# Second-level products and accumulating DMAs in the first pair of a cross-network kernel

## Chip, cores, metric

The kernel runs on one core of one Trainium2 chip. The metric is the device time of one execution in microseconds (us). The time before is 2277.18 us (median of 3 runs, 2277.13 to 2278.06).

## The reference, cut to what matters

```python
# x0: 16384 x 1024 bf16, ws: 6 x 1024 x 1024 bf16, bs: 6 x 1024 bf16
x = x0
for l in range(6):
    proj = jnp.einsum('bd,de->be', x, ws[l]) + bs[l]
    x = x0 * proj + x
```

## The kernel before

The 16384 rows are done in 16 pairs of two blocks of 512 rows; a pair goes through six layers, so there are 96 layer passes. Each pass multiplies by a 1024 x 1024 matrix in Winograd's form of Strassen's scheme: seven products with half-size blocks, called 1 to 7, instead of eight. Four of the seven need a sum of weight blocks. Such a sum is the same for all 16 pairs, so the first pair (pair 0) makes it on VectorE and saves it to DRAM (`Lc`); the other 15 pairs only load it. Pairs 1 to 15 also cut products 5 and 2 a second time into seven quarter-size products ("two levels"). Their weight sums are called 5i and 2i and are made in pair 0 as well.

```python
RING = 16                                         # weight tiles of 0.52 MB
level1 = lambda u: units[u][0] == 0 or u == NU - 1    # pair 0 and the last pass: one level
RAW = [("4", "load"), ("w12", "stage"), ("1", "load"), ("2", "load")]
MAKE = [(w, "make") for w in ("5", "6", "7", "3")]
...
            combo("5", "w12", "4", ADD, ())       # on VectorE, then saved
            combo("6", "5", "1", SUB, ("5",))
            combo("7", "1", "w12", SUB, ())
            combo("3", "2", "6", SUB, ("6",))
            for X, s in (("2i", isum[2 * (l % 2)]), ("5i", isum[2 * (l % 2) + 1])):
                icombo("5", lambda a=a, sv=sv: tt(sv[:, 0], a(0, 1), a(1, 1), ADD), ())
                icombo("6", lambda a=a, sv=sv: tt(sv[:, 1], sv[:, 0], a(0, 0), SUB), "5")
                icombo("3", lambda a=a, sv=sv: tt(sv[:, 2], a(1, 0), sv[:, 1], SUB), "6")
                icombo("7", lambda a=a, sv=sv: tt(sv[:, 3], a(0, 0), a(0, 1), SUB), ())
                save(X, lambda s=s: s, [rn(i) for i in "5637"])
```

Every operation carries a rank, which is its planned time in microseconds from the start of its layer. The program is emitted in the order of these ranks, and each engine (SyncE, which issues most DMAs, GpSimd, which issues the rest, ScalarE, VectorE, TensorE) works off its own list strictly in that order. An operation that is not ready holds all later ones of its engine, whatever they need.

## Time and profile before

| | kernel before |
|---|---|
| time, median of 3 runs | 2277.18 us |
| span of the profiled run | 2275.2 us |
| TensorE / VectorE / ScalarE busy | 100% / 91% / 81% |
| DMA issues in pair 0 from GpSimd | 36 plain saves, 6.2 and 6.9 us to landing (median) |

This is the table by stretch of the kernel before. Behind the stretch stand its length and, for PE (TensorE), PEld (its weight loads), DVE (VectorE), ACT (ScalarE) and POOL (GpSimd), the busy microseconds with the number of instructions; then come the granted TensorE clock, the busy share of the DMA engines, and what they moved in GB/s.

```profile
20.00:60.00 40.00, 39.63 (x184) 18.00 (x184) 39.06 (x46) 28.08 (x48) 8.17 (x12) 1.00 0.86 305
60.00:100.00 40.00, 40.00 (x187) 18.09 (x185) 39.10 (x45) 27.31 (x48) 4.76 (x9) 1.00 0.83 227
100.00:140.00 40.00, 40.00 (x187) 18.16 (x186) 38.92 (x43) 27.14 (x47) 3.71 (x7) 1.00 0.60 207
```

TensorE never stops and runs at full clock, VectorE is nearly full, and the DMA engines are busy 60 to 86% of the time. (Shares a little over 1 occur, as overlapping packets are both counted.) From 17 to 150 us the share is 0.75 on average, so some 33 us of DMA time are idle there. That is the room into which the change puts its new transfers.

### The profile page before, as it was taken

The page shows a single profiled execution, that of the slowest core. Times are in us where ns is not written, and L with a number is a line of the kernel's source. Part 1 is how long each engine was busy: PE and PEld are TensorE (multiplying, and loading weights), DVE is VectorE, ACT ScalarE, POOL GpSimd, SP SyncE. Part 2 cuts the span into 40 slices and gives each one's busy share as a digit, 9 for nine tenths or more (in the row PEclk, how much of TensorE's full clock was granted, in tenths as well). Part 3 has the DMA queues.
Part 4 walks back from the last instruction along what each step waited for, and adds up shares of the span by engine and source line. Part 5 has one row for each costly group of instructions (what it writes and reads, how often), then busy time and mean ns, then how long its engine had stood idle before and what let it go on. Part 6 is the DMA issues. An engine that isn't in the chain of part 4 may idle for free.

```text
span 2275.2 us, 34978 instructions
## 1 busy us (share of the span) xinstructions
PE 2265.4 (100%) x12951; PEld 1264.0 (56%) x12951; DVE 2079.9 (91%) x2326; ACT 1839.4 (81%) x3228; POOL 22.1 (1%) x43
## 2 busy tenths in 40 slices
PE   9999999999999999999999999999999999999998
PEld 4455555555555555555555555555555555555554
DVE  7999999999999999999999999999999999999997
ACT  5678888888888888888888888888888888888887
POOL 1110000000000000000000000000000000000000
PEclk9999999999999999999999999999999999999999
DMA  9779797796977969779697796978969689696872
GB/s 279 229 270 289 261 242 269 219 301 209 252 257 221 288 217 260 250 226 283 213 274 241 228 283 204 273 245 230 283 200 292 226 232 286 194 303 216 241 240 65
DMA packets 625868, 557.01 MB, mean 245 GB/s; under 512 B 397600, under 2 KB 552224, under 8 KB 625696
## 3 DMA queue, kind: packets, MB, share of 16 engines
q1 hardware_dynamic: 618864, 534.58, 79.1%
q0 software_dynamic: 5184, 18.88, 2.2%
q8 instruction: 101, 1.65, 0.3%
q10 hardware_dynamic: 1648, 1.32, 0.2%
q14 instruction: 71, 0.58, 0.1%
HBM read 436.22 MB, written 52.43 MB: 215 GB/s over the span
## 4 chain that ended last, share of the span: by engine, by line
PE 98%; DVE 1%; SPq 0%; DMA 0%; issue 0%; ACT 0%; DVEq 0%
PE pA L285 57%; PE pX L389 24%; PE pX L285 16%; DVE ev L198 1%; SPq L529 0%; DMA wp<-in_ws_dram 0%; DVE xst L198 0%; DVE T L198 0%; DVE ti L198 0%; DVE wp L198 0%; SPq L538 0%; ACT ev L294 0%; DVE x0T L487 0%; DVEq L608 0%; DVEq L198 0%
## 5 line engine op out<-in xcount | busy, mean ns | idle before, releaser
L285 PEld LDWEIGHTS <-wp 128*128 128x128 bf16 x7904 | 772.3, 98 | 843.7 <-issue 3.9
L285 PE MATMUL pA<-T,wp 128*128 128x512 bf16 x4608 | 1054.9, 379 | 0.5 <-DVE T L198 0.5
L294 ACT ACTIVATE ev<-pA,b_all 128x512 bf16<-128x512 f32 x1124 | 704.8, 690 | 211.8 <-PE pA L285 211.4
L389 PEld LDWEIGHTS <-wp 128*128 128x128 bf16 x4984 | 487.1, 98 | 156.6 <-issue 15.2
L198 DVE TENSOR_TENSOR ev<-ev,x0T 128x2048 bf16<-128x2048 bf16 (+2 forms) x484 | 482.7, 999 | 8.1 <-ACT ev L294 1.5
L198 DVE TENSOR_TENSOR xst<-ev,xst 128x2048 bf16<-128x2048 bf16 x319 | 388.9, 1219 | 18.6 <-DVE ev L198 0.5
L389 PE MATMUL pX<-ti,wp 128*128 128x256 bf16 x2848 | 397.6, 272 | 0.0
L198 DVE TENSOR_TENSOR ev<-ev,ev 128x2048 bf16<-128x2048 bf16 (+1 forms) x283 | 343.7, 1215 | 26.7 <-ACT ev L294 9.8
L294 ACT ACTIVATE ev<-pX,b_all 128x512 bf16<-128x512 f32 x412 | 289.4, 705 | 59.9 <-PE pX L285 49.3
L285 PE MATMUL pX<-xst,wp 128*128 128x512 bf16 x1376 | 336.4, 379 | 0.0
L285 PE MATMUL pA<-xst,wp 128*128 128x512 bf16 x1280 | 313.5, 379 | 0.0
L290 ACT COPY pX<-pA 128x512 f32<-128x512 f32 x412 | 256.3, 625 | 44.7 <-PE pA L285 44.3
L290 ACT CAST ev<-pX 128x512 bf16<-128x512 f32 x384 | 224.8, 619 | 49.0 <-ACT ev L294 37.6
L198 DVE TENSOR_TENSOR ev<-iu,ip 128x1024 bf16<-128x1024 bf16 x178 | 122.4, 688 | 120.7 <-ACT iu L290 120.7
L290 ACT COPY pX<-pX 128x512 f32<-128x512 f32 x356 | 208.7, 587 | 8.4
L290 ACT CAST iu<-pX 128x512 bf16<-128x512 f32 x356 | 196.8, 639 | 0.0
L198 DVE TENSOR_TENSOR T<-xst 128x2048 bf16<-128x2048 bf16 x160 | 194.8, 1217 | 0.3
L198 DVE TENSOR_TENSOR T<-xst,T 128x2048 bf16<-128x2048 bf16 x160 | 194.5, 1216 | 0.0
L389 PE MATMUL pX<-T,wp 128*128 128x256 bf16 x1068 | 160.2, 273 | 0.0
L290 ACT CAST ip<-pX 128x512 bf16<-128x512 f32 x178 | 104.7, 589 | 54.1 <-PE pX L389 54.1
L389 PE MATMUL pX<-xst,wp 128*128 128x256 bf16 x888 | 133.2, 273 | 0.0
L198 DVE TENSOR_TENSOR xst<-ev,x0T 128x2048 bf16<-128x2048 bf16 x64 | 78.2, 1222 | 1.6
(44 smaller groups left out, 624.3 us busy)
## 6 DMA issues: line engine op xcount, KB each, us to landing
wp<-Lc SPq DMA_DIRECT2D x538, 512.0 KB, 4.6
wp<-in_ws_dram SPq DMA_DIRECT2D x285, 512.0 KB, 5.3
out_dram<-x0T SPq DMA_DIRECT2D x30, 1024.0 KB, 8.6
Lc<-wp POOLq DMA_DIRECT2D x24, 512.0 KB, 6.2
Lc<-isum POOLq DMA_DIRECT2D x12, 512.0 KB, 6.9
w<-in_ws_dram SPq DMA_DIRECT2D x5, 512.0 KB, 6.3
wp<-in_ws_dram ACTq DMA_DIRECT2D x2, 512.0 KB, 5.8
out_dram<-x0T SPq DMA_DIRECT2D x2, 512.0 KB, 3.6
```

What stands on the lines that cost most here:

```text
L198: nc.vector.tensor_tensor(out=o, in0=a, in1=b, op=op)
L285: nc.tensor.matmul(bank[:], lhsT=wt[(u, w)][:, k, m * P:(m + 1) * P], rhs=rhs[:, k, :], start=(start and k == 0), stop=(k == KH - 1), skip ...
L290: add(name, lambda: nc.scalar.copy(out=dst, in_=src), rd, wr)
L294: add(name, lambda: nc.scalar.activation(out=dst, in_=src, func=IDENT, bias=b_all[:, c:c + 1], scale=1.0), rd, wr)
L389: nc.tensor.matmul(pX[bank][:, m * NQ:(m + 1) * NQ], lhsT=wv[:, k, m * P:(m + 1) * P], rhs=rhs[:, k, :], start=(start and m == 0 and k == ...
```

## The change

In layers 2 to 5 of pair 0 the change goes to two levels, as the later pairs do. VectorE has no time for that, so the weight sums of these layers move to the DMAs. A base block is loaded (SyncE), where needed ScalarE changes its sign, and then GpSimd issues an accumulating DMA that adds a second block to it: 5 = w12 + w4, 7 = -w12 + w1, 6 = -w4 + (7), 3 = w2 + (6). Of the small sums for the second level, two of four are done in the same way on quarter blocks. Layers 0 and 1 stay at one level, and all ranks of pair 0 are new. The saves move from GpSimd to SyncE. Weight 4 gets two buffers of its own, and weights w12 (layers 0 and 1), 7 and 6 (layer 2) lie in `xst` memory that pair 1 uses later. The diff, cut to its core:

```diff
+    NONE = 2
-    level1 = lambda u: units[u][0] == 0 or u == NU - 1
+    level1 = lambda u: u < NONE or u == NU - 1
+    ADDED = [(w, "load") for w in ("5", "2", "7", "6", "3", "1")] + [("4", "four")]
+    BASE = {"5": "w12", "7": "w12", "6": "4", "3": "2"}
...
-                    nc.gpsimd.dma_start(Lc[l, CIDX[w]]...            # saves
+                def fn(eng=nc.gpsimd if first and len(w) == 1 else nc.sync):
...
+                for w in "76":
+                    for h in range(2):
+                        add(f"n{w}.{h}", ... nc.scalar.activation(... func=IDENT, scale=-1.0), ...)
+                def accum(w, src, more=(), weights=()):
+                    add("d" + w, ... nc.gpsimd.dma_start(out=raw(w)[:], in_=src(), accum_op=ADD), ...)
+                accum("5", lambda l=l: w_src(l, "4"))
+                accum("7", lambda l=l: w_src(l, "1"))
+                accum("6", lambda raw=raw: raw("7")[:], [f"w{u}.7"], "7")
+                accum("3", lambda raw=raw: raw("6")[:], [f"w{u}.6"], "6")
...
+                        add(X + i + "l", ... nc.sync.dma_start(dst(), part(w)), [], [rn(i)])
+                        if X == "5i":
+                            add(X + i + "a", ... nc.gpsimd.dma_start(out=dst(), in_=part("4"), accum_op=ADD), ...)
+                        add(X + i + "m", ... nc.gpsimd.dma_start(out=dst(), in_=more(), accum_op=ADD), ...)
... (the new ranks of all layers of pair 0 are left out)
```

## The prediction

> **What bounds the kernel now.** I read the page first (busy shares), then the chain of work that ended last, then tables of busy time by stretch, then the groups of instructions, and last the timeline of TensorE at the start. The page says PE busy 100%, DVE 91%, ACT 81%, and that the chain that ended last is 98% PE. A busy PE is only a bound if its matmuls follow each other at their own pace, so I take the pace from the chain (columns: start, duration, what):
>
> ```profile
> 68.87 10.36 PE pA L285 x48
> 93.05 10.36 PE pA L285 x48
> 117.22 10.36 PE pA L285 x48
> ...
> 1766.37 8.63 PE pA L285 x40
> 1789.81 8.63 PE pA L285 x40
> ```
>
> 48 matmuls of 512 columns take 10.36 us, so 0.2158 us each. The same place of two neighbouring layers of the first pair lies 117.22 - 93.05 = 24.17 us apart: this is 112 x 0.2158 = 24.17, seven products of 16 matmuls with no gap. In a later pair, where products 5 and 2 are cut once more, the distance is 1789.81 - 1766.37 = 23.44 us (80 full matmuls and 56 of 256 columns). So a layer costs 24.17 us with one level and 23.44 us with two, and each is pure TensorE time.
>
> Stalls exist only at the very start (TensorE's timeline; the bracket is idle time before it and what ended it):
>
> ```profile
> 12.81 2.85 PE L285 MATMUL pX<-x0T,wp 128*128 128x512 bf16 x12 [1.26 <-ACT pX L290]
> ...
> 17.98 1.90 PE L285 MATMUL pX<-T,wp 128*128 128x512 bf16 x8 [0.49 <-DVE wp L198]
> 20.36 10.52 PE L285 MATMUL pA<-T,wp 128*128 128x512 bf16 x48 [0.49 <-DVE T L198]
> 30.72 3.62 PE L285 MATMUL pX<-x0T,wp 128*128 128x512 bf16 x16
> 34.17 3.62 PE L285 MATMUL pA<-xst,wp 128*128 128x512 bf16 x16
> ```
>
> Layer 0 runs from 6.78 to 34.17 us, 27.4 us for 24.2 us of matmuls. After that nothing holds TensorE until the tail. Whether it can go to two levels earlier is a question for VectorE and the DMAs (table by stretch: length, busy time and count of each engine, clock, DMA share, GB/s; a layer of the first pair, then one of the second):
>
> ```profile
> core 0: us, PE busy (x) PEld busy (x) DVE busy (x) ACT busy (x) POOL busy (x), PEclk, DMA share, GB/s
> 117.20:140.60 23.40, 23.40 (x111) 10.56 (x109) 22.90 (x26) 16.56 (x28) 1.07 (x2) 1.00 0.53 169
> 188.40:211.90 23.50, 23.50 (x134) 12.95 (x133) 21.29 (x24) 20.13 (x36) 0.00 (x0) 1.00 1.14 253
> ```
>
> VectorE is busy 22.90 of 23.40 us in the first pair: it makes the weight combinations beside the layer's own sums. That is why the first pair has one level only.
>
> **What the Trainium skill says.** "TensorE: Matmul & The Clock Gate", section "Wait — 56ns, not 53.3ns?", gives 215.7 ns start to start for 512 columns at full clock; the trace agrees (0.2158 us, granted clock 1.00). "VectorE: DVE Perf Modes", section "The perf-mode tier table (the rule you actually need)", gives 1224 ns for a 2048-element bf16 two-tensor operation; the trace has 1217 ns for a weight combination. "DMA: Bandwidth & Descriptors", section "SWDGE vs HWDGE vs iDMA", says an accumulate during a DMA can only be issued from GpSimd, and its subsection "Issuing engines are not separate DMA queues" that all issuers share the same 16 DMA engines. No accumulating DMA is in this trace, so its price is not measured; that is the weakest spot here.
>
> **The change part by part.** Layers 0 and 1 stay at one level and are re-ordered; layers 2 to 5 of pair 0 get two levels.
>
> 1. TensorE, removed: 4 layers x (24.17 - 23.44) = 4 x 0.73 = 2.9 us. All of it is on the path, as there are no gaps there.
>
> 2. VectorE. The groups with shapes kept apart:
>
> ```profile
> L198 DVE TENSOR_TENSOR wp<-wp 128x2048 bf16<-128x2048 bf16 x12 | 14.6, 1217 | 0.0
> L198 DVE TENSOR_TENSOR isum<-wp 128x512 bf16<-128x512 bf16 x24 | 9.8, 417 | 1.8 <-DMA wp<-in_ws_dram 1.8
> ```
>
> A layer has four large combinations and eight small ones. In a row they start some 1.14 and 0.34 us apart in the timeline, so 4 x 1.14 + 8 x 0.34 = 7.3 us per layer. The change leaves four small ones (1.4 us) and takes 5.9 us away. Two levels add the six operations that prepare the second level's inputs (2 x (0.60 + 0.34 + 0.34) = 2.6 us), two closing sums (2 x 0.60) and one full sum (1.14), together 4.9 us. VectorE thus ends about 1 us lower in a layer that is 0.7 us shorter: still some 95% busy. Without the move to DMA it would need about 28 us in 23.4 us. So the move is what makes the second level possible; by itself it saves no time.
>
> 3. ScalarE: 6 more evictions (34 for 28) and 4 sign changes of 128 x 1024. The second pair's layer shows 20.13 us busy of 23.50 us; four sign changes of about 1 us (estimate from 690 ns for 512 columns) come to 24 us when counted in full, but these records overlap: evictions start 0.5 to 0.6 us apart, so about 34 x 0.55 + 4 = 23 us at most. Tight, but the negations lie up to two layers ahead, and those of layers 2 and 3 partly in one-level layers (16.56 us busy).
>
> 4. DMA, added per layer 2 to 5: loads go from 4 to 7 of 0.52 MB plus four quarter parts (+2.1 MB); four accumulates of 0.52 MB and six of 0.13 MB (2.9 MB). That is 5 MB a layer, 20 MB in all. In the stretch from 17 to 150 us the old kernel moved 240 GB/s x 133 us = 32 MB at share 0.75. 52 MB in some 131 us is 395 GB/s. In the stretch 150 to 179 us, with its DMAs busy all the time, the old kernel reached 388 GB/s, with pieces of 400 to 430. So the DMA engines go from 75% to full in the first pair, even if an accumulated byte costs no more than a copied one. If it costs double (it reads both operands), 12 MB more, about 28 us of DMA time, are in demand.
>
> 5. Small waits that I expect by following the new order: the change frees no time in layer 0, whose first 13.6 us hang on the arrival of x0 and of the two weight quarters as before, so its 3.2 us of stall stay. In layer 1, VectorE does 23 operations from the last half combination (17.9 us) to the layer's T1, 23 us of work plus dependent pairs that start 1.25 instead of 1.14 us apart; T1 is ready 0.3 to 0.4 us after TensorE has finished products 1 and 2 at 41.1 us. Layer 2 begins with inner products that want the difference of T1 early: another 0.4 us. Layers 3 to 5: together 0.3 us. Sum about 1.1 us.
>
> 6. Not touched: 89 later layers (23.44 us each), the last layer and the tail. Moving weight 4 to its own two buffers gives the ring one free place, but TensorE never waits for a weight there, so it is worth 0.
>
> Sum: -2.9 + 1.1 = -1.8 us, from 2277.2 to 2275.4 us.
>
> **The rivals.** (a) The DMA engines become the bound in the first pair. For it: step 4, and two transposing loads of x0 that fall into layer 3 and block the SyncE queue for 20 us in the old timeline. Against it: accumulates are issued 10 us or more ahead of their use (layers 3 to 5: 12 to 20 us by the order's ranks), saves of combinations are due only in the second pair, and the ring of 16 weights gives two layers, some 46 us, of lead. A backlog of 10 us would vanish there; one of 30 to 40 us (the doubled price) would stall TensorE late in pair 0 and early in pair 1 by perhaps 2 to 10 us: 2278 to 2286 us. (b) Head-of-line blocking: GpSimd's and SyncE's queues now hold waits for each other (load, negate, accumulate, accumulate from the result, save). One late link delays all behind it; VectorE too, as 5i7 of layer 2 reads an accumulated weight. I expect 0 to 3 us. (c) All is hidden and the small waits of step 5 do not come: 2277.2 - 2.9 = 2274.3 us. (d) VectorE stays the hidden bound and the two-level layers run at its pace: it would have to lose more than 1 us per layer to waits; up to +2 us.
>
> **Range and chances.** I give the clean outcome (2274.3 to 2276) about 60%, small stalls (2276 to 2280) 25%, a real DMA shortage 15%. The weighted middle is a little over the sum: 2275.9 us, eight in ten between 2274.0 and 2281.5 us. Two per cent are 45.5 us; the whole gain in sight is 2.9 us, so faster by over 2% is nearly excluded (0.003), and slower by over 2% would need the first pair's 145 us to grow by a third (0.012). Within 2%: 0.985.
>
> **What would show it right or wrong.** Right: layers 2 to 5 lie 23.4 to 23.9 us apart on TensorE; VectorE's operations that write wp drop from 25 (two of them halves) to 9; DMA share near 1 from 30 to 150 us; TensorE's waits over 17 us sum to about 1.1 us more than now and name DVE T or ti. Step 4 is wrong if accumulates of 0.52 MB land within 7 us and the share stays under 0.9; rival (a) is right if TensorE waits for the DMA of wp or isum, above all in layers 4 to 6; rival (b), if VectorE or ScalarE waits for a DMA while the DMA share is below 1. The prediction fails if accumulates run far slower than copies, or if the second pair starts with its ring empty.

## The result

The changed kernel takes 2351.04 us (median of 4 runs, 2339.95 to 2353.0), beside 2277.62 us of the kernel before in the same rounds. The ratio is 1.031, with a 95% interval of 1.028 to 1.034. (A ratio here is the mean time of one kernel's fast runs over the mean of the other's of the same rounds, so it is not quite the ratio of the medians quoted.) The result is correct. The change costs 73 us; the prediction was 2275.9 us with 2274.0 to 2281.5 as its range, so it was wrong. The profiled run is the fastest of the four: its span is 2338.1 us, 62.9 more than before.

**Where the time went.** The chain of work after pair 0 has the old pace: the same long run of TensorE starts at 304.74 and at 1782.46 us, 63 layers apart, which is 23.46 us per layer (before: 242.07 and 1766.37 us, 65 layers, 23.45 us). From 242.07 to 304.74 is 62.7 us, so all of the loss lies before 305 us. The table by stretch of the changed kernel:

```profile
20.00:60.00 40.00, 38.20 (x177) 17.09 (x176) 37.48 (x46) 31.91 (x53) 21.66 (x15) 1.00 1.13 323
60.00:100.00 40.00, 22.84 (x120) 12.15 (x119) 18.03 (x24) 15.61 (x27) 11.62 (x11) 0.80 1.05 282
100.00:140.00 40.00, 15.39 (x69) 8.12 (x69) 15.64 (x18) 16.08 (x25) 8.87 (x8) 0.64 1.23 234
140.00:180.00 40.00, 35.31 (x193) 19.01 (x192) 30.35 (x38) 31.08 (x54) 9.92 (x9) 0.96 1.13 288
```

Now the DMA engines are the ones that never stop (share over 1 in every row), while TensorE works 38 of 80 us in the two middle rows. Note the last number: full DMA engines move only 234 to 323 GB/s here. The kernel before moved 388 GB/s with full engines (150 to 179 us).

TensorE's stalls are few and long. These lines are from its timeline (start, duration, what, and in brackets the idle time before it and what ended it):

```profile
69.30 1.01 PE L455 MATMUL pX<-ti,isum 128*128 128x256 bf16 x4 [8.05 <-DVE ti L216]
...
107.52 5.55 PE L313 MATMUL pA<-T,w 128*128 128x512 bf16 x16 [15.51 <-ACT ev L322]
...
134.22 1.01 PE L455 MATMUL pX<-T,wp 128*128 128x256 bf16 x4 [15.50 <-ACT pX L318]
172.28 3.01 PE L313 MATMUL pX<-xst,wp 128*128 128x512 bf16 x8 [4.69 <-DMA wp<-wp]
192.57 1.04 PE L455 MATMUL pX<-ti,isum 128*128 128x256 bf16 x4 [5.90 <-DMA isum<-wp]
```

These five sum to 49.7 us; with the smaller ones the idle time from 15 us on is 55.5 us, where the kernel before had 1.0 us. That is 54.5 us more, less 2.9 us for the saved matmuls, so 51.6 of 62.9 us. The other 11 us, by subtraction, are slow matmuls after each stall: the timeline lines that follow the five stalls are 10.5 us longer than the same groups at full clock. In the lines shown, 16 matmuls of 512 columns take 5.55 us at 107.52 and 3.62 us at full clock; 4 of 256 columns take 1.01 instead of 0.60 us. The Trainium skill describes this ("TensorE: Matmul & The Clock Gate", section "What's actually happening": after an idle window of about 3.4 us the array falls back to half clock until it has been busy again). The trace agrees: the granted clock is 0.80 and 0.64 in the two rows with the long stalls and 1.00 before them.

Only the last two of the five stalls name a DMA. For the others one has to go one step back, to what ScalarE, VectorE and SyncE waited for in this time (who waited for what: total us, times, longest):

```profile
ACT wp L365 <- DMA wp<-in_ws_dram: 21.0, 3, 16.3
ACT wp L365 <- issue: 15.3, 1, 15.3
DVE ti L216 <- DMA Lc<-ti: 7.7, 1, 7.7
SPq L274 <- DMA Lc<-wp: 34.0, 11, 10.3
SPq L399 <- DMA Lc<-isum: 22.2, 2, 19.0
```

L365 is the sign change. ScalarE stands 36 us before sign changes whose block has not been loaded, and the evictions that TensorE needs stand behind them in its list. ("issue" means that the profile names no releaser. By the program this wait, too, can only be for a block: the load issued at 121.05 us landed at 131.96, and the sign change began at 132.04.) The 8 us of VectorE are of the same kind: it may not overwrite a tile `ti` before its save has landed.

SyncE (SPq), which issues the loads (L274, L399), was held in two ways. Ahead of the second stall it waited for saves to land so that their buffers were free (56 us in all, 19.0 of them from 62 to 81 us); the load that the second stall waits for was issued at 88.08 us, after this, and took 15.6 us to land. Ahead of the third stall it was the issuing itself: from 92 to 122 us SyncE waited for saves for only 2 us, but its 11 issues took 27.7 us. The view of the line (times of one issue in ns, shortest, median and longest) shows it:

```profile
L274 SPq DMA_DIRECT2D wp<-in_ws_dram x8: 387/1160/9939, 88.1 to 121.1; - x8
```

In the kernel before, the same issues from 17 to 150 us took 0.37 to 1.6 us each. So the roots of all five stalls are transfers that come late, or whose issue does. They come late because a transfer now takes long (this is the list of DMA issues from 20 to 200 us, median us from issue to landing last):

```profile
Lc<-wp SPq DMA_DIRECT2D x14, 512.0 KB, 14.5
Lc<-isum SPq DMA_DIRECT2D x8, 512.0 KB, 16.5
wp<-in_ws_dram POOLq DMA_DIRECT2D x7, 512.0 KB, 13.8
wp<-wp POOLq DMA_DIRECT2D x6, 512.0 KB, 15.2
```

A save that took 6.2 us before takes 14.5 us (GpSimd issued it then and SyncE does now; no run moves the saves back, so what that alone costs is not known), and the accumulates (the two POOLq lines) take 13.8 and 15.2 us.

### The profile page after: what moved, and what is told of

It reads as the page before. It is cut to its first block, busy times and chain, and to the rows that moved or that the text cites. A ratio compares the mean times of both kernels' runs of the same rounds, so it can differ in the third digit from the quotient of the medians.

```text
span 2338.1 us, 35331 instructions
## 1 busy us (share of the span) xinstructions
PE 2275.2 (97%) x13047; PEld 1276.4 (55%) x13047; DVE 2078.2 (89%) x2330; ACT 1866.7 (80%) x3268; POOL 56.6 (2%) x51
## 2 busy tenths in 40 slices
DMA packets 647438, 576.96 MB, mean 247 GB/s; under 512 B 398688, under 2 KB 572768, under 8 KB 647264
## 4 chain that ended last, share of the span: by engine, by line
PE 92%; DMA 4%; SPq 1%; issue 1%; DVE 1%; POOL 0%; ACT 0%; DVEq 0%; POOLq 0%; ACTq 0%
PE pA L313 54%; PE pX L455 24%; PE pX L313 14%; DMA isum<-in_ws_dram 1%; DMA wp<-xst 1%; DMA isum<-wp 0%; SPq L274 0%; DMA Lc<-xst 0%; DVE ev L216 0%; SPq L595 0%; DMA xst<-xst 0%; DMA Lc<-isum 0%; SPq L399 0%; DMA w<-in_ws_dram 0%; DVE wp L216 0%
## 5 line engine op out<-in xcount | busy, mean ns | idle before, releaser
L313 PEld LDWEIGHTS <-wp 128*128 128x128 bf16 x6208 | 607.8, 98 | 649.3 <-issue 10.0
L322 ACT ACTIVATE ev<-pA,b_all 128x512 bf16<-128x512 f32 x1140 | 716.5, 691 | 203.1 <-PE pA L313 202.8
L313 PE MATMUL pA<-T,wp 128*128 128x512 bf16 x3040 | 718.9, 379 | 0.5 <-DVE T L216 0.5
L455 PEld LDWEIGHTS <-wp 128*128 128x128 bf16 x5080 | 496.8, 98 | 178.7 <-issue 33.1
L313 PE MATMUL pA<-T,w 128*128 128x512 bf16 x1536 | 350.3, 381 | 16.9 <-ACT ev L322 16.9
L313 PE MATMUL pX<-xst,wp 128*128 128x512 bf16 x1312 | 323.5, 380 | 5.7 <-DMA wp<-wp 4.7
L322 ACT ACTIVATE ev<-pX,b_all 128x512 bf16<-128x512 f32 x396 | 278.1, 707 | 62.5 <-PE pX L313 52.9
L318 ACT COPY pX<-pA 128x512 f32<-128x512 f32 x396 | 247.9, 628 | 27.9 <-PE pA L313 27.6
L313 PEld LDWEIGHTS <-w 128*128 128x128 bf16 x1536 | 150.8, 98 | 199.4 <-issue 20.2
L318 ACT COPY pX<-pX 128x512 f32<-128x512 f32 x372 | 218.1, 587 | 9.3 <-PE pX L455 0.3
L318 ACT CAST iu<-pX 128x512 bf16<-128x512 f32 x372 | 207.3, 638 | 1.0 <-PE pX L455 0.9
L455 PE MATMUL pX<-T,wp 128*128 128x256 bf16 x1100 | 165.6, 273 | 15.6 <-ACT pX L318 15.5
## 6 DMA issues: line engine op xcount, KB each, us to landing
Lc<-wp SPq DMA_DIRECT2D x18, 512.0 KB, 11.1
wp<-in_ws_dram POOLq DMA_DIRECT2D x7, 512.0 KB, 13.8
wp<-wp POOLq DMA_DIRECT2D x6, 512.0 KB, 15.2
```

The source lines that it names most:

```text
L313: nc.tensor.matmul(bank[:], lhsT=wt[(u, w)][:, k, m * P:(m + 1) * P], rhs=rhs[:, k, :], start=(start and k == 0), stop=(k == KH - 1), skip ...
L318: add(name, lambda: nc.scalar.copy(out=dst, in_=src), rd, wr)
L322: add(name, lambda: nc.scalar.activation(out=dst, in_=src, func=IDENT, bias=b_all[:, c:c + 1], scale=1.0), rd, wr)
L455: nc.tensor.matmul(pX[bank][:, m * NQ:(m + 1) * NQ], lhsT=wv[:, k, m * P:(m + 1) * P], rhs=rhs[:, k, :], start=(start and m == 0 and k == ...
```

## The experiments

All kernels of a batch ran on one chip beside the kernel before, whose median was 2276.8 to 2277.4 us in every batch; e3_probe was run once and serves as a profile only. The changed kernel itself was not run again, and its four runs lie between 2339.95 and 2353.0 us, so a difference against its median is uncertain by some 10 us. Letters for theories in the expectations were given run by run; the text after each says in words which account its numbers belonged to. Kernels marked "wrong" compute wrong weight sums. They still pass the comparison, as the projections are small beside x0.

My account was: (1) an accumulated byte costs the DMA engines far more than a copied one, so that in pair 0 they lack some 60 us, and TensorE pays nearly all of it. Its rivals: (2) the engines' in-order lists hold each other up, whatever a byte costs; (3) the sign changes on ScalarE; (4) single buffers that are too few.

### What an accumulating DMA costs by itself: e3_probe

The kernel before, with batches of four DMAs of 0.52 MB at its end, when nothing else runs: copies from DRAM, accumulates from DRAM, accumulates from on-chip memory, copies from on-chip memory, twice over. After each batch VectorE waits for all four.

```diff
+        for t, i in zip(tiles, srcs):
+            nc.gpsimd.dma_start(out=t[:], in_=i, accum_op=ADD)      # and without accum_op
+        ... (VectorE reads one element of each tile, then writes one)
+        for t, i in zip(tiles, isum):
+            nc.gpsimd.dma_start(out=t[:], in_=i[:], accum_op=ADD)   # and without accum_op
```

> The kernel before, with batches of four DMAs of 0.52 MB from GpSimd after its end, one batch at a time: copies from HBM, accumulates from HBM, accumulates from SBUF, copies from SBUF, twice. Theory A: a batch of accumulates takes 11-14 us, a batch of copies 6-8 us, with nothing else on the DMA engines. Theories B and C: both 6-8 us, and the slow accumulates in the changed kernel are only queueing behind other transfers. The result stays right, the time grows by the batches, some 80 us.

VectorE's timeline; the idle time in brackets is the time of one batch:

```profile
2290.88 0.16 DVE L595 COPY ev<-ev 128x1 bf16<-128x1 bf16 x1 [14.38 <-DMA ev<-in_ws_dram]
...
2304.12 0.16 DVE L602 COPY ev<-ev 128x1 bf16<-128x1 bf16 x1 [12.71 <-DMA ev<-isum]
...
2311.85 0.16 DVE L609 COPY ev<-ev 128x1 bf16<-128x1 bf16 x1 [7.21 <-DMA ev<-isum]
...
2322.01 0.16 DVE L588 COPY ev<-ev 128x1 bf16<-128x1 bf16 x1 [9.63 <-DMA ev<-in_ws_dram]
```

L595 and L602 close the accumulates, L609 and L588 the copies. From DRAM a batch takes 14.4 against 9.6 us (1.5 times), on-chip 12.7 against 7.2 us (1.8 times). In slices of 2.1 us the DMA rate is about 195 GB/s in the accumulates (204 at most) and reaches 353 to 405 GB/s in the copies, so about half. GpSimd also needs 1.3 us to issue an accumulate from DRAM and 0.75 us for a copy. So the price that the prediction had not measured is about double in DMA rate.

### The accumulates made plain copies: e1_plain (wrong)

```diff
-nc.gpsimd.dma_start(out=raw(w)[:], in_=src(), accum_op=ADD)
+nc.gpsimd.dma_start(out=raw(w)[:], in_=src())        # and the same in both small accumulates
```

> Every accumulating DMA of the changed kernel copies plainly (same bytes, same queues and waits; the result is wrong on purpose). Theory A, an accumulated byte costs over twice a copied one and so the DMA engines run out: 11.5 MB at 168 GB/s (68 us) become 11.5 MB at some 378 GB/s (30 us), 38 us of DMA time go, and the time falls from 2351 to 2300-2315 us. Theory B, blocked in-order queues (ScalarE's negations, SyncE's waits) whatever the DMAs cost: 2335-2352 us. Theory C, the added bytes alone: 2340-2352 us.

It took 2311.27 us (ratio 1.015), within the 2300 to 2315 us of the first account: every transfer, wait and order is kept, and 39.8 of 73 us are gone by the medians (29.1 of 62.9 us between the two profiled runs). This is what the accumulating itself costs, its longer issue on GpSimd included. GpSimd's queue carries the same bytes in both kernels; the DMA queue lines from 20 to 200 us (packets, MB, time of its packets as a share of the 16 engines' 180 us), first of the changed kernel:

```profile
q0 software_dynamic: 11409, 13.60, 44.3%
```

and of the one with copies:

```profile
q0 software_dynamic: 4032, 13.63, 20.2%
```

That is 79.7 us against 36.4 us of DMA time, 43 us less, for 39.8 us of kernel time by the medians and 29.1 us by the profiled runs, from which the 43 us are read. 2.1 MB of the queue are plain saves, some 5.6 us at 378 GB/s (the rate of this queue's packets in the kernel before). The remaining 11.5 MB thus cost 74 us accumulated and 31 us copied: **2.4 times the price**. The packet time of the probe's batches tells how much of this is the accumulating alone. Here are the second batch of accumulates from DRAM (a window of 14.3 us) and the second of copies (9.7 us):

```profile
q0 software_dynamic: 2112, 2.10, 95.0%
q0 software_dynamic: 576, 2.10, 61.9%
```

That is 13.6 against 6.0 us, 2.3 times; on-chip it is 11.1 against 5.3 us, 2.1 times. (The 1.5 and 1.8 above are lower because a batch also holds 0.5 to 3.6 us without packets, most in the copies from DRAM.) At these prices the 11.5 MB, of which 5.2 come from DRAM, would cost about 67 us accumulated and 31 us copied, by estimate; so some 7 of the 74 us came with the traffic beside them. The larger number of packets is not the main cause: on-chip it stays at 576 a batch, and the price doubles all the same.

### Fewer bytes: e4_nosave, e6_inner_dve

e4_nosave leaves out the saves of layers 2 to 5 (wrong: later pairs read the sums of layers 0 and 1), 12.6 MB or about 33 us at 378 GB/s. The accumulates stay.

```diff
+                if l >= NONE:
+                    return            # in save()
-        return Lc[l, CIDX[w]]...
+        return Lc[l % NONE, CIDX[w]]...
```

> The saves of layers 2 to 5 (24 of 0.52 MB, 12.6 MB) are left out and later pairs load those of layers 0 and 1 (wrong result on purpose); the accumulates stay. Theory A or C, DMA time is what is short: 12.6 MB at 350-378 GB/s are 33-36 us, so 2308-2322 us. Theory B with ScalarE's negations as the cause: no more than 10 us, 2340-2352 us. (It takes SyncE's waits for saves away as well, so it does not tell those from the DMA time.)

e6_inner_dve puts the small second-level sums back on VectorE (right result), behind the one that was there already. This takes away four quarter loads and six small accumulates per layer, 5.2 MB in all.

```diff
+icombo("5", lambda a=a, sv=sv: tt(sv[:, 0], a(0, 1), a(1, 1), ADD), ())
+icombo("3", lambda a=a, sv=sv: tt(sv[:, 2], a(1, 0), sv[:, 1], ADD), "6")
-(the loads X+i+"l" and the accumulates X+i+"a", X+i+"m")
```

> The changed kernel with all small second-level weight combinations back on VectorE (16 quarter loads and 24 small accumulates go, 16 VectorE operations of 0.34 us come). Account of A: 6.3 MB more loads (17 us) and 8.4 MB of accumulates (54 us) against 33 us of idle time leaves 38 us, less 2.9 us of matmuls: 2305-2320 us. If instead the small accumulates only mattered by their latency, or VectorE were now the bound, 2335-2352 us. Result right.

e4_nosave took 2322.75 us (1.020), 28 us less than the change, just outside the range of 2308 to 2322 that the first account gave. e6_inner_dve took 2314.17 us (1.016), 37 us less, within the 2305 to 2320 of the first account. There the accumulating queue's packet time fell from 79.7 to 55.3 us (30.7% of 180 us) and 2.1 MB of loads (5.5 us) went too, about 30 us. Three different ways of taking 43, 33 and 30 us of DMA time away thus give 40, 28 and 37 us of kernel time by the medians, and 29, 19 and 26 us between the profiled runs, in which the DMA times were read: 0.6 to 1.2 us for each us, so DMA time is paid for the most part. (e4_nosave also takes away SyncE's waits for saves, so it alone doesn't tell the two apart; e1_plain does.) Of the versions with all four layers and a right result, e6 is the best; no run joins it with the order of e14 below.

### Both removed: e8_plain_nosave (wrong)

The edits of e1_plain and e4_nosave together: 76 us of DMA time less, more than the missing 60 us.

> Both earlier cuts together, plain copies in place of accumulates and no saves of layers 2 to 5 (wrong result on purpose); ScalarE's negations, the quarter loads, all waits between queues and the two-level order stay. Account of A: 22 us of loads and 31 us of copies, less 33 us of saves, is 20 us, under the 33 us of idle time: no DMA shortage, 2274-2280 us. Theory B: the stalls of about 12 us behind ScalarE's waits stay, 2288-2305 us.

It took 2303.82 us (1.011), still 26.6 us over the kernel before. My account had expected 2274 to 2280 us, so it is not the whole; the rival's 2288 to 2305 held. The largest stall left is of the kind that ScalarE makes:

```profile
111.69 1.01 PE L457 MATMUL pX<-T,wp 128*128 128x256 bf16 x4 [14.69 <-ACT pX L318]
```

ScalarE waited 14.9 us there for the load of a block whose sign it is to change.

### The sign changes: e2_noneg, e12_e8_noneg (wrong)

```diff
-                for w in "76":
+                for w in "":          # no sign changes
```

e2_noneg is the changed kernel with this edit, e12_e8_noneg is e8_plain_nosave with it.

> The 16 sign changes on ScalarE are left out (wrong result on purpose), so ScalarE waits for no load of a weight; all DMAs stay. Theory A: the DMA engines are as full as before, 2330-2352 us. Theory B with ScalarE's queue as the cause: the two stalls of TensorE of 15.5 us behind a negation go and are not made up elsewhere, 2305-2322 us.

> As e8_plain_nosave, without the 16 negations (wrong result on purpose). Theory D, ScalarE's in-order queue is what turns a late load into a stall of TensorE: the same 14.7 us go, 2283-2291 us. If the late load would hold TensorE anyway (by the weights' own arrival): 2297-2306 us.

e2_noneg took 2345.11 us (1.030), 6 us less than the change, whose own runs scatter over 13 us; beside the 8.3 us of the first, its stalls merely changed their names (13.6, 14.1, 6.1, 6.4 and 6.9 us, now for DMAs and VectorE). e12_e8_noneg took 2296.54 us (1.0085), 7 us less than e8, between the two ranges expected. So the third account is worth 6 to 7 us either way. The sign changes are where ScalarE met the shortage, not its cause.

### Buffers and order in the changed kernel: e7_third_isum, e11_x0late, e14_queue_fixes, e18_e14_save_early (right results)

Each of these removes one hold in SyncE's list. e7: layer 3's small sums get a pair of buffers of their own, for which SyncE had waited 19 us. e11: the two transposing loads of pair 2's x0, which took SyncE 25 us in the middle of the shortage (20 us before the change), go one layer later. e14: both, and weight 4's load stands behind the next layer's first four loads. e18: e14, with the save of layer 0's 5i ahead of a load of layer 3.

```diff
+iset = [spare[:, 0], spare[:, 1]] if l == 3 else [t[:] for t in isum[2 * (l % 2):2 * (l % 2) + 2]]   # e7
-if l == (2 if pr == 0 else 0) and nxt < NPAIR:   ... op(base + 23 + n, ld, [], XN)
+if l == (3 if pr == 0 else 0) and nxt < NPAIR:   ... op(base + (30 if pr == 0 else 23) + n, ld, [], XN)   # e11
+    for u in range(NONE + 1, L - 1):                                                                     # e14
+        ring_seq.remove((u, "4", "four"))
+        ring_seq.insert(ring_seq.index((u + 1, "6", "load")) + 1, (u, "4", "four"))
-... s5i@38.12
+... s5i@36.00                                                                                           # e18
```

> The changed kernel with a third pair of buffers for the second-level combinations, for layer 3, so SyncE does not wait for the save of layer 1's before it loads layer 3's quarters (19 us in the trace of the changed kernel, with all later loads behind it). Theory A: DMA work is the same, the wait is filled by other transfers: 2335-2352 us. Theory B with SyncE's queue as the cause: that wait goes, 2318-2334 us. Result right.

> The changed kernel itself with the transposing loads of x0 moved as in e10. Theory A for the full change: its DMA engines are full from 20 to 200 us, so moving work in time gains little, 2335-2355 us. If the transposes' hold of SyncE's queue (25 us in its trace) were a main cause beside the price of accumulating: 2320-2333 us. Result right.

> The changed kernel with the same three changes of SyncE's queue, accumulates and saves as they are (result right). Theory A for the DMA time: 96 us of added DMA time against 33 us of idle leave it far above the kernel before whatever the queues do, 2310-2332 us. If the queues were most of it and accumulates would hide: under 2300 us.

> The changed kernel, right result, with the three queue mendings (2327.5 us) and the same earlier save. There VectorE waited 18.3 us for that save. Account (accumulates and saves keep the DMAs short of time, so most of what one wait gives back is taken by the next one for the DMAs): 2315 to 2328 us. Rival (the queue order is what costs, the price of an accumulate does not matter): below 2305 us, within 20 us of the run with plain copies and no saves.

| kernel | median us | ratio | against the change |
|---|---|---|---|
| e7_third_isum | 2347.47 | 1.031 | -4, within its scatter |
| e11_x0late | 2331.99 | 1.024 | -19 |
| e14_queue_fixes | 2327.47 | 1.022 | -24 |
| e18_e14_save_early | 2328.06 | 1.022 | -23 |

The loads of x0 are the one hold that is worth much, and that was the miss among these: my account had put e11 at 2335 to 2355. These edits give 23 us by order and buffers alone; the other 50 us stay. e18 lies at the upper edge of the 2315 to 2328 us of my account: VectorE's wait for the save, 18.3 us in e14, is gone in it, and the time is the same, as ScalarE's waits for loads (18.7 and 12.2 us) took its place.

### Order where bytes are cheap: e10_e8_x0late, e13_e8_four_later, e16_e8_queue_fixes, e17_e16_save_early (wrong)

The same edits on e8_plain_nosave: e10 moves the loads of x0, e13 the load of weight 4, e16 does these two and the buffers of e7, e17 moves the save of 5i as well.

> As e8_plain_nosave, with the two transposing loads of the second pair's x0 issued one layer and 7 us later (wrong result on purpose). In e8's trace one stall of 14.7 us is left that matters most: ScalarE's negation waits for a weight load issued just before these transposes. Theory D: that stall goes with its clock loss, 2283-2291 us, unless the transposes hold another load there. If the stall has another cause: 2299-2308 us.

> As e8_plain_nosave (wrong result on purpose), with the load of weight 4 of layers 3 and 4 placed behind the next layer's loads of 5, 2, 7 and 6 in SyncE's queue. Theory F (that load's wait for product 4 of two layers before holds the loads that ScalarE's negations wait for): the stall of about 14 us and its clock loss go, 2285-2293 us. If the late loads are late for another cause: 2299-2306 us.

> As e13 (wrong result on purpose), with the third pair of second-level buffers and the later loads of x0 as well: no known hold of SyncE's queue is left, copies in place of accumulates, no saves of layers 2 to 5. Theory F: 2278-2288 us, only the 5 us late start of layer 2 and small waits are left. If order and queues were not the rest: 2295-2305 us.

> As the run with plain copies, no saves and the three queue mendings (2294.5 us, 17.3 over the kernel before), but the save of layer 0's second-level sums 5i stands ahead of layer 3's quarter load in SyncE's queue (36.00 for 38.12). There that save was issued at 60.0 us behind the quarter load, which waited 5.4 us for its place, and VectorE waited 9.39 us for the save before it could overwrite the tile with layer 2's sums; TensorE lost 9.76 us. Account (what is left without a DMA shortage is made of single in-order waits like this one): 2280 to 2289 us, the 9.8 us stall gone or under 3 us, and a further 1 to 3 us of half clock with it. Rival (the rest is spread over many small causes, or the next wait takes over at once): 2290 to 2296 us.

They took 2302.40, 2299.83, 2294.49 and 2294.31 us (ratios 1.0111, 1.0100, 1.0076, 1.0076): 1.4, 4.0, 9.3 and 9.5 us less than e8. Neither the x0 loads nor weight 4's place explains the rest (I had expected at most 2291 and 2293 us for e10 and e13), and e16 missed the 2278 to 2288 us that I had given it. e17 is the most telling miss: it had 2280 to 2289 us, and its rival's 2290 to 2296 us held. In e16 one stall stood out, on TensorE and then on VectorE, which waited for the save of a tile:

```profile
70.69 1.01 PE L462 MATMUL pX<-ti,isum 128*128 128x256 bf16 x4 [9.76 <-DVE ti L216]
```

```profile
69.94 0.69 DVE L216 TENSOR_TENSOR ti<-T 128x1024 bf16<-128x1024 bf16 x1 [9.39 <-DMA Lc<-ti]
```

With the save moved ahead by one place, that wait is gone in e17; VectorE does this operation at 60.99 us without a pause. But the time did not move by 1 us, as ScalarE now waits before two sign changes:

```profile
82.37 1.06 ACT L370 ACTIVATE wp<-wp 128x1024 bf16<-128x1024 bf16 x1 [5.84 <-DMA wp<-in_ws_dram]
...
102.05 1.06 ACT L370 ACTIVATE wp<-wp 128x1024 bf16<-128x1024 bf16 x1 [7.87 <-DMA wp<-in_ws_dram]
```

By the ranks, the first of these belongs to a weight of layer 4, while TensorE is at the end of layer 2 and waits for the evictions behind it. The table by stretch of e17 shows why those loads were late:

```profile
20.00:60.00 40.00, 38.73 (x179) 17.25 (x178) 38.67 (x47) 32.98 (x54) 19.10 (x16) 1.00 1.07 365
60.00:100.00 40.00, 30.93 (x160) 16.22 (x160) 31.91 (x40) 25.15 (x41) 8.51 (x13) 0.90 1.07 365
100.00:140.00 40.00, 35.77 (x204) 20.79 (x204) 29.23 (x38) 34.72 (x60) 9.64 (x15) 0.89 0.71 220
```

Until 100 us the DMA engines are full even with plain copies and without the late saves; after that they are not (0.71). From 20 to 100 us they moved 365 GB/s x 80 us = 29 MB, the kernel before 305 x 40 + 227 x 40 = 21 MB. By the ranks, the blocks of layers 2 and 3 are loaded and added to one to two layers ahead, beside the saves of layers 0 and 1, and in that stretch there is no room, although over the whole of pair 0 there is. What the runs leave open is how much of the last 17 us is this early demand and how much is the order alone: no run made the one vanish without the other.

### One layer only: e5_layer5, e9_layer5_early, e15_layer5_order (right results)

If the account is right, one changed layer should fit into the 33 us of idle DMA time. By the measured prices it needs 2.1 MB of loads (5.6 us at 378 GB/s) and 74 / 4 = 18.5 us of accumulates, 24 us. e5 is the kernel before with the change in layer 5 alone; e9 makes layer 5's sums two layers earlier; e15 also gives layer 4 the order that the changed kernel has in layer 1 (a one-level layer with a two-level layer behind it), and makes small sums of layers 2 and 3 earlier.

```diff
+    NONE = 5                                         # e5
-d5@-31.65 d7@-27.05 ...   n6.0@-45.40 n7.1@-29.65 ...
+d5@-71.0 d7@-66.0 ...     n6.0@-69.0 n7.1@-71.0 ...  # e9
-(layer 4) P1.1@.04 P1.0@.90 ...
+(layer 4) P1.1@-1.18 P1.0@-.31 ...                   # e15: the changed kernel's order of layer 1
```

> The kernel before with the change in layer 5 alone (layers 0 to 4 one level, as before). The account of theory A: one layer adds 2.1 MB of loads (5.6 us of DMA time at 378 GB/s) and 2.9 MB of accumulates (18.5 us, a quarter of 74), 24 us; the kernel before leaves a quarter of the 133 us from 17 to 150 idle, 33 us. 24 is less than 33, so nothing stalls and one layer's gain of 0.7 us is left: 2275.9-2277.0 us. Theory B, the chains of waits in in-order queues stall any such layer: 2283-2295 us. Result right.

> As e5_layer5, but everything of layer 5 that needs no late buffer (loads of its three sums, the quarter loads, the negations, accumulates d5, d7, d6 and three small ones) is moved ahead into layer 2, where the DMA engines stand idle (59 to 69 us). Trace of e5: a load delayed by the transposing loads of x0 held a negation for 4.1 us on ScalarE, then TensorE 2.9 us, its clock, then VectorE 5 us, and layer 5 began late. Theory D (the total of DMA time suffices for one layer, but a load that is late at one place holds an in-order queue, and VectorE, 95% busy, never makes it up): 2275.9-2277.5 us. Theory B in its strict form (the chain of loads, negations and accumulates stalls wherever it lies): 2283 us or more. Result right.

> As e9_layer5_early, but layer 4 has the order that the change gives to the one-level layer ahead of a two-level one (so that the sums that T1 of layer 5 needs come early), and the late small combinations of layers 2 to 4 come earlier. In e9's trace TensorE waited 3.4 us at layer 5's first inner product and 2.9 us where VectorE waited for a save. Theory D with fitting orders: 2276-2280 us. If one two-level layer costs more than its 0.7 us under any order: 2284 us or more. Result right.

They took 2291.27, 2287.22 and 2282.40 us (ratios 1.0061, 1.0044, 1.0020). My account had expected about 2276 us for e5 and missed it; the other side's 2283 to 2295 us held. e9, for which I had again given about 2276 us, stayed above 2283 us too, so loading earlier does not settle it by itself; e15 fell between the 2276 to 2280 us of one answer and the 2284 or more of the other. A single layer costs 14 us if added as it stands, and 5 us with a place and an order made for it. In e15 the DMA share is 0.93, 1.11 and 0.76 in the three stretches from 20 to 140 us, and no stall of TensorE names a DMA any more; the largest left are

```profile
115.53 3.63 PE L302 MATMUL pX<-T,wp 128*128 128x512 bf16 x15 [1.50 <-DVE T L204]
...
142.18 1.02 PE L302 MATMUL pA<-T,xst 128*128 128x512 bf16 x4 [1.16 <-DVE T L204]
```

waits for VectorE of 1 to 2 us, as in step 5 of the prediction but larger. So for one layer the DMAs no longer stop TensorE directly. It still loses 5 us there, where it could have gained 0.7 us. No version beats the kernel before.

## Why the prediction was wrong

**Right:** Step 1. The trace has 96 more matmuls, 4 x (136 - 112), and the later layers keep their pace. Step 2. VectorE's operations that write weight sums fell from 25 to 9, as said, and VectorE was not the bound. Step 6. The later pairs are untouched. The amount of data in step 4 was right too: the pages count 576.96 MB in place of 557.01, 20 MB more, as said.

**The step that failed is step 4 with rival (a): the price of an accumulate, and what a shortage costs.** The prediction said that the DMA engines go to full "even if an accumulated byte costs no more than a copied one", and that doubled cost would put about 28 us more of DMA time in demand. Nothing in the trace before showed the price, which the text called its weakest spot, and yet the clean outcome got 60%. Measured: 2.4 times in packet time (74 us for 11.5 MB against 31 us), 2.1 to 2.3 times in the probe alone. With 43 us more, not 28, pair 0 needs 4 x 24 = 96 us of DMA time where 33 us were idle: 63 us short, worked out from the measured prices; the profiled run lost 62.9 us and the median run 73 us. That these agree so well is partly chance, since the loss also has parts that order can mend.

The second half of the same step was worse. The prediction held that a backlog of 30 to 40 us would cost "perhaps 2 to 10 us", because accumulates are issued early and the ring holds two layers of weights. Measured, the whole loss is 63 us in the profiled run and 73 in the median, and three experiments give 19 to 40 us for 30 to 43 us of DMA time. The lead of the ring did not help; my reading, which no run tests by a longer lead, is that it is filled by the same engines, so that any lead is eaten once they are full for 100 us. And a stall costs more than itself, as TensorE then runs at half clock for some microseconds, 11 us in all here.

**Rival (b) was right in kind and far too small.** The prediction gave head-of-line waits 0 to 3 us. Mending the order gave 23 us in the changed kernel (e14, e18). With cheap bytes and no late saves 27 us are left, of which mending gives 10. The test that I had set for telling (a) from (b), whether an engine waits for a DMA "while the DMA share is below 1", could not do so: the share was over 1 nearly all the time and the long waits were in the lists of ScalarE and SyncE. Both happen at once, as a list that holds turns a late transfer into a stall of engines that do not need it.

**Step 3** counted ScalarE's busy time and found it tight but enough. The sign changes took 1.06 us each, as estimated. What it missed is that a sign change waits for a load, and that evictions due now stand behind it: 36 us of waiting. Taking the sign changes away gave only 6 to 7 us, so this is a place where the shortage shows more than a cause.

**Step 5** was about right for layers 0 and 1: from 15 to 45 us TensorE is idle for 1.06, 0.49 and 0.28 us. **Rivals (c) and (d)** are out: TensorE stalls for 55 us, and in the two stretches with the long stalls VectorE works only 18.0 and 15.6 of 40 us. One sum is loose: with the middles of its own three brackets the prediction's weighted middle is about 2276.9 us and not 2275.9, which changes nothing here.

A page that I had not looked up bears on this: the Trainium skill, "Collectives: The Full Stack", section "The bandwidth ceiling: the fold count and why AG ≠ RS ≠ AR", says of the adding DMAs in a collective that an add needs two source reads, and measures the collective that copies at 1.93 times the rate of the one that adds. Whether a kernel's accumulating DMA works in that way no run here shows, but the rates of e3_probe, 195 against 353 to 405 GB/s, are in line with it. It would have been ground for taking the doubled price as the expected case and not as a rival with 15%.

## What to carry to other kernels

Before sums are moved from VectorE to accumulating DMAs, measure one batch of such DMAs beside the same copies, and count them at two to two and a half times their bytes. Compare that DMA time with the idle DMA time of the very stretch in which it has to happen, not of the whole stage, and take a shortage as paid for the most part (0.6 to 1.2 us for each us here): do not count on prefetch when the engines that prefetch are the ones that are full. Where engines work in order, an operation that waits for a DMA must not stand ahead of work that is due now; and if removing one such wait does not move the time, look at the next one before believing that it was harmless.

## What the Trainium skill lacked or had wrong

- "DMA: Bandwidth & Descriptors" says where an accumulating DMA can be issued but gives no price. Here four of 0.52 MB took 14.4 us against 9.6 us for copies from DRAM and 12.7 against 7.2 us on-chip, and 2.1 to 2.3 times the packet time, 2.4 times in the kernel. "Collectives: The Full Stack" has a ratio of 1.93 for collectives only; the runs are in line with it for a kernel's own DMAs.
- "DMA: Bandwidth & Descriptors" has no issue cost on GpSimd for an accumulate: 1.3 us from DRAM, 0.75 us for a copy (e3_probe). Beside full DMA engines the groups of accumulates took 1.1 to 1.8 us on average to issue, and a GpSimd copy of one column took 9.3 us where it had taken 2.3 us in the kernel before.
- No page that I read has how long an issue on SyncE itself takes while the DMA engines are full. Here one issue of a 0.52 MB load took up to 9.9 us (0.37 to 1.6 us in the kernel before), and the two issues of the transposing loads held SyncE for 25 us (20 us before); moving these two by one layer gave 19 us in the changed kernel and 1 us where bytes were cheap.
